# A gated mix of a long convolution and a token-mixing MLP: DFT tables laid out by group of four shifts, and a new emission order

## Chip, core and metric

The kernel runs on one core of a Trainium2 chip. The metric is the device time of one execution in microseconds. The engines are TensorE (PE, with weight loads as PEld), VectorE (DVE), ScalarE (ACT), GpSimd (POOL) and SyncE (SP); here SP issues every DMA. Shown are 13 runs of the kernel before, and one profiled execution.

## What is computed

For an input x of 2048 tokens by 640 channels, the kernel computes `g*a + (1-g)*b`, with g a sigmoid gate for each token. Branch a is a long convolution; branch b is a mixer with two residual steps:

```python
x = A_q
g = sigmoid((x * gate_w).sum(-1, keepdims=True))
# a
k_shift = sum over t<4 of shifted k * shift_k
kv = k_shift * v
y = irfft(rfft(kv, 2S) * rfft(ssm_k, 2S))[:S]
a = q * (y + kv * ssm_D)
# b
h = gelu(layernorm(x) @ w1)
hs = concat(four channel groups of h, shifted by 1, -1, 2, -2 tokens) @ w2
x1 = x + hs
b = x1 + gelu(layernorm(x1) @ w3) @ w4
```

Inputs and output are bf16; the transform in the reference is f32.

## The kernel before

**Tiling.** Tokens are laid out as 128 partitions by 16 slabs (`T1 = 16`), so that a slab is a tile of 128 tokens by 640 channels. The slabs of x are held in QX and updated in place. Branch b runs in four chunks of four slabs; branch a transforms along the tokens in two steps, one over the partitions of each slab and one over the slabs.

**Nodes.** The work is cut into named nodes, each with its engine, its dependencies and its buffers. The text of `ORDER` lists all nodes in the order in which they are emitted; `h1.6.1/P/2/1`, say, is node `h1.6.1` on PE, with PSUM bank 2 and store buffer 1. `Plan.order` reads this text and emits each node at its place. An engine works through its own nodes in that order, and waits wherever one needs something that isn't ready. The costs given to `pl.add` and `pl.dma` (`rate`, `iss`, `ndesc`) are for the planner that wrote the text; no instruction depends on them.

**Branch b.**
- `st0`, `rs0`, `xn0` (L497 to L530): layernorm statistics, their power, the normalized slab. `tr`/`te` transpose it on PE, or `xt` (L537) by DMA, into XNT.
- `W1.c.n` (L574): first matmul, five column groups for chunk c; `g1` (L581) is its gelu. `gt.c` (L588) is the gate's matmul and `z` its evacuation, `gate0` to `gate2` the sigmoid.
- `mx.c.gi` (L609 to L614): copies of 32 partitions that shift the rest of the four channel groups; they run on POOL or on DVE.
- `W2.s` (L663) and `add.s` (L670): second matmul of a slab and its sum into QX, which also gives the second layernorm's sums. Then `st1`, `rs1`, `xn1`, and `xt1` (L537).
- `W3.c.f` (L749), `g2` (L753), `W4.s.j` (L762), `w4e.s.j` (L768): the last two matmuls, the gelu between them, and the sum into QX. `xo.s` scales a slab by 1-g. The load of w4 (L733) waits for `m3n`, since it overwrites the place in which M3 is made.

**Branch a.**
- `ang`, `and`, `sin`, `abs` (L391 to L405) make the first DFT table F1, with half h (0 and 1, the table's two halves of 128 columns) and slab s. They work in four groups of four slabs; each group is two sines and an abs on ScalarE. The angles are kept in the tile of the inverse table, I1, until it is filled.
- `trh`/`trhe` transpose the convolution's kernel. `h1.s.h` (L718) is its first DFT step for slab s and half h, two matmuls; `he` evacuates them and `hw` (L727) stores two slabs to GHD in DRAM.
- `km`, `ka`, `kv` (L806 to L818): the short convolution of k and the product with v, on DVE. `x1.s.h` (also L718), `xe`, `xw` do for kv what `h1`, `he`, `hw` do for the kernel, to GXD.
- `m3i`, `m3b`, `m3c` (L432 to L448), `m3d` (L452), `m3s` (L454), `m3n` (L456): the small second-step table M3, made on POOL but for m3b and m3d on DVE and a sine on ScalarE.
- `rh`/`rx` (L862) read GHD and GXD back in another order; `h2`, `x2` (L835) are the second step, `sw` swaps halves, `pq` (L895) multiplies, `pv` goes back; `ve` and `vw` (L912) store to VD.
- `tri0`, `tri1` (L824): two DMA transposes that fill I1 from F1, one for each half. `rv` (L919), `rq` (L923), `iv` (L931), `ye`, `y`, `ya` (L941 to L951) and `st` (L953): read VD, inverse first step, times q and gate, sum, and store of a slab.

PSUM has eight banks, and there are rings of buffers for the stores (sg, 3), the gelu outputs (gt, 4) and more. A node that takes a buffer waits for the users of the one that had this place before.

**What the change touches.** F1 and I1 are tiles of 128 partitions by [2 halves, 16 slabs, 128 columns]. The sines of group g write columns of every second place in both halves:

```python
F1 = big.tile([P, 2, T1, P], BF16, name="F1")
out=F1[:, :, 4 * g:4 * g + 4, :].rearrange("p h a (j c) -> p a h j c", c=2)[:, :, :, :, x]
```

In `step1` the matmul reads `F1[:, h, s, :]`. Both transposes wait for all eight sines and for m3n, and each inverse node waits for both transposes.

Of the kernel before, what the change touches and what calls it, by code (L numbers as in the profile page):

```python
# [34 lines left out]
class Plan:  # L35
# [17 lines left out]
    def dma(self, name, fn, nbytes, deps=(), bufs=(), rate=370.0, iss=360.0, ndesc=128):  # L53
        return self.add(name, {"SP": iss}, fn, deps, bufs, None, nbytes, rate, iss, ndesc)
# [31 lines left out]
bpi/V q1/S is/G cs/V iw/G cw/V ang3/V and3/V sin3.1/A ang1/V and1/V sin1.1/A abs1/A ang2/V idn/G warm/P/0 h0/S trh0/P/2 q0/S  # L86
st0.0/A st0.3/V st0.2/V trhe0/A/2 ang0/V and0/V st0.1/V misc/G rs0.2/G xn0.3/V/0 xn0.2/V/1 h4/S trh4/P/4 trhe4/V/4 rs0.0/G
xn0.1/V/2 h1/S trh1/P/6 sin1.0/A trhe1/A/6 sin0.1/A abs0/A sin0.0/A tr0.0.2/P/0/0/1/0 xn0.0/V/0 and2/V te0.0.2/V/0/0 sin2.1/A
h3/S trh3/P/2 tr0.0.0/P/4/0/0/2 te0.0.0/V/4/0 q3/S st0.7/V st0.6/V w1/S W1.0.3/P/0/0 W1.0.2/P/1/0 w1m/G trhe3/V/2 q2/S st0.5/V
st0.4/A h2/S g1.0.3/A/0 trh2/P/6 g1.0.2/A/1 trhe2/V/6 rs0.6/G q7/S xn0.6/V/1 xn0.7/V/0 rs0.4/G W1.0.0/P/2/0 xn0.4/V/2  # L90
W1.0.4/P/3/0 g1.0.4/A/3 mx0.0/G kz/G/0 h1.1.1/P/4/0 he.1.1/A/4/0 h1.5.0/P/6/1 he.5.0/V/6/1 tr0.1.2/P/0/1/1/0 te0.1.2/A/0/1
ka/S/0 g1.0.0/A/2 xn0.5/V/0 q5/S st0.11/V gw/S gt.0/P/3/0 w2b2/S h1.5.1/P/4/1 he.5.1/A/4/1 q6/S q4/S st0.12/A tr0.1.0/P/6/1/2/0
te0.1.0/V/6/1 st0.10/V m3i3/G rs0.10/G W1.0.1/P/0/0 h1.4.0/P/4/1 he.4.0/A/4/1 h1.4.1/P/6/1 he.4.1/V/6/1 g1.0.1/A/0 W1.1.0/P/1/1
g1.1.0/A/1 W1.1.4/P/2/1 g1.1.4/A/2 h1.2.0/P/6/2 he.2.0/A/6/2 st0.9/V z0/V/3 w2b0/S w2a/S kb/S/0 drow/S h1.0.1/P/4/0
he.0.1/A/4/0 h1.0.0/P/0/0 he.0.0/A/0/0 W1.1.1/P/3/1 w2b3/S cjb/S w2b1/S hw2/S/1 mx1.1/G xn0.10/V/1 xt0.2.2/S/0/1 st0.8/V
xn0.11/V/0 xt0.2.3/S/0/0 kc/S/0 st0.15/V h1.3.1/P/6/2 he.3.1/A/6/2 h1.3.0/P/4/2 he.3.0/V/4/2 abs3/A g1.1.1/A/3 W1.1.3/P/2/1
g1.1.3/A/2 h1.1.0/P/0/0 h1.2.1/P/6/2 m3i0/G he.2.1/A/6/2 rs0.8/G xn0.8/V/2 xt0.2.0/S/0/2 st0.13/V he.1.0/V/0/0 W1.1.2/P/4/1
g1.1.2/A/4 hw0/S/0 xn0.9/V/1 mx1.0/G xt0.2.1/S/0/1 h1.7.0/P/2/1 he.7.0/A/2/1 st0.14/V gt.1/P/5/1 z1/V/5 h1.7.1/P/6/1
he.7.1/A/6/1 abs2/A sin3.0/A sin2.0/A mx1.3/G mx0.2/G W2.5/P/0 add5/V/0 hw1/S/2 rs0.12/G xn0.13/V/0 xn0.12/V/2 xt0.3.1/S/1/0
st1.5/A h1.6.0/P/2/1 mx0.1/G h1.6.1/P/4/1 he.6.0/A/2/1 he.6.1/V/4/1 hw3/S/1 W2.3/P/6 add3/V/6 st1.3/A W2.2/P/0 add2/V/0 st1.2/A  # L100
cj3/G cj1/G m3i5/G W2.4/P/4 add4/V/4 rs0.14/G xn0.15/V/1 xt0.3.0/S/1/2 xt0.3.3/S/1/1 h1.12.1/P/6/0 W1.2.1/P/0/0 m3b/V
g1.2.1/A/0 gt.2/P/1/0 h1.13.0/P/2/0 W1.2.2/P/4/0 W1.2.4/P/5/0 km0.0.3/V/0/0 xn0.14/V/0 st1.4/A xt0.3.2/S/1/0 g1.2.2/A/4
g1.2.4/A/5 z2/V/1 he.12.1/V/6/0 h1.11.0/P/0/2 he.11.0/A/0/2 he.13.0/V/2/0 h1.13.1/P/6/0 he.13.1/A/6/0 W1.2.3/P/4/0
h1.12.0/P/2/0 h1.9.1/P/0/1 he.12.0/A/2/0 he.9.1/A/0/1 W1.2.0/P/5/0 v0/S h1.8.1/P/6/1 gt.3/P/0/1 he.8.1/A/6/1 h1.10.1/P/2/2
he.10.1/A/2/2 cj2/G cj0/G hw6/S/0 km0.0.2/V/0/0 ka0.0.2/V/0/0 rs1.2/G xn1.2/V/2 xt1.0.0/S/0/2 km0.0.1/V/0/1 km0.0.0/V/0/0
ka0.0.1/V/1/0 z3/V/0 ka0.0.0/V/0/0 g1.2.0/A/5 g1.2.3/A/4 W1.3.2/P/1/1 h1.9.0/P/6/1 h1.10.0/P/2/2 he.9.0/A/6/1 he.10.0/A/2/2
W1.3.4/P/0/1 g1.3.4/A/0 kv0/V/0 mx2.3/V km0.1.3/V/0/0 xn1.3/V/1 rs1.4/G xn1.5/V/0 mx2.1/G km0.1.2/V/0/1 mx1.2/V km0.1.1/V/0/0
W1.3.1/P/4/1 g1.3.1/A/4 g1.3.2/A/1 h1.14.1/P/6/0 he.14.1/A/6/0 W1.3.3/P/0/1 h1.8.0/P/2/1 g1.3.3/A/0 h1.15.1/P/4/0 he.15.1/A/4/0
xn1.4/V/2 ka0.1.2/V/1/0 he.8.0/V/2/1 W1.3.0/P/1/1 h1.14.0/P/6/0 he.14.0/A/6/0 ka0.1.1/V/0/0 gate0/V m3i2/G mx2.0/G W2.9/P/4
h1.11.1/P/2/2 g1.3.0/A/1 m3i4/G m3i1/G m3c/G he.11.1/A/2/2 gate1/A mx3.1/G m3d/V m3s/A km0.1.0/V/0/1 mx3.2/G m3n/G add9/V/4  # L110
h1.15.0/P/6/0 W2.6/P/0 he.15.0/A/6/0 w3/S W2.8/P/2 gate2/V ka0.1.0/V/1/0 xo2/A add6/V/0 W2.7/P/4 kv2/V/0 xt1.0.3/S/0/0 add8/V/2
xt1.0.1/S/0/1 xt1.0.2/S/0/2 W3.0.3/P/0/0/0 W3.0.4/P/1/0/1 W3.0.2/P/2/0/0 g2.0.2/A/2/0 g2.0.3/A/0/0 st1.6/A W3.0.9/P/3/0/2
g2.0.4/A/1/1 W3.0.8/P/6/0/2 g2.0.8/A/6/2 W3.0.1/P/7/0/0 W3.0.7/P/0/0/1 g2.0.9/A/3/2 W3.0.5/P/1/0/1 W3.0.11/P/6/0/2 g2.0.5/A/1/1
g2.0.1/A/7/0 g2.0.11/A/6/2 add7/V/4 st1.7/A k1/S/1 km1.0.3/V/1/0 km1.0.2/V/1/0 ka1.0.2/V/0/0 km1.0.1/V/1/1 ka1.0.1/V/1/0
km1.0.0/V/1/0 ka1.0.0/V/0/0 v1/S st1.9/A xo4/A kv4/V/0 km1.1.3/V/1/0 km1.1.2/V/1/1 ka1.1.2/V/1/0 km1.1.1/V/1/0 km1.1.0/V/1/1
ka1.1.1/V/0/0 mx3.0/G mx2.2/G mx3.3/G W3.0.0/P/1/0/0 W2.11/P/4 W3.0.6/P/2/0/1 W2.12/P/6 ka1.1.0/V/1/0 kv6/V/0 W3.0.10/P/3/0/2
g2.0.7/A/0/1 add11/V/4 rs1.6/G st1.8/A g2.0.6/A/2/1 hw4/S/1 k2/S/0 km2.0.3/V/0/0 w4/S km2.0.2/V/0/0 v3/S W2.10/P/4 v2/S
ka2.0.2/V/0/0 hw5/S/2 tri0/S rs1.8/G xn1.9/V/0 xo9/V g2.0.0/A/1/0 g2.0.10/A/3/2 st1.11/A xo3/A W4.3.0/P/0/0/1/2
W4.3.1/P/1/0/1/2 x1.3.0/P/2/1 xe.3.0/A/2/1 add10/V/4 st1.10/A xn1.6/V/1 xn1.8/V/2 xt1.1.2/S/1/2 xt1.1.3/S/1/0 km2.0.1/V/0/1
ka2.0.1/V/1/0 w4e3.1/V/1 w4e3.0/V/0 k3/S/1 xt1.1.0/S/1/1 km2.0.0/V/0/0 ka2.0.0/V/0/0 rs1.10/G W4.2.0/P/4/0/1/2 w4e2.0/V/4  # L120
x1.0.1/P/2/2 xe.0.1/A/2/2 kv8/V/0 W2.13/P/0 add13/V/0 xn1.11/V/2 km2.1.3/V/0/0 km2.1.2/V/0/1 xn1.7/V/0 W4.4.1/P/2/0/1/2
x1.2.0/P/4/1 xe.2.0/A/4/1 add12/V/6 ka2.1.2/V/1/0 W4.2.1/P/3/0/1/2 w4e4.1/V/2 xo11/A st1.12/A xn1.10/V/1 km2.1.1/V/0/0 st1.13/A
xo5/V x1.0.0/P/0/2 W4.5.1/P/4/0/1/2 W4.5.0/P/2/0/1/2 ka2.1.1/V/0/0 km2.1.0/V/0/1 w4e2.1/V/3 hw7/S/0 xt1.1.1/S/1/0
W4.4.0/P/5/0/1/2 w4e4.0/V/5 W3.1.2/P/3/1/3 g2.1.2/A/3/3 W3.1.7/P/5/1/0 g2.1.7/A/5/0 x1.1.1/P/6/2 W3.1.0/P/3/1/3 xe.0.0/A/0/2
xe.1.1/A/6/2 W3.1.3/P/5/1/3 g2.1.0/A/3/3 g2.1.3/A/5/3 rs1.12/G xn1.13/V/0 xo13/V ka2.1.0/V/1/0 kv10/V/0 xt1.2.0/S/0/1 tri1/S
km3.0.3/V/1/0 xt1.2.3/S/0/0 w4e5.0/V/2 km3.0.2/V/1/0 x1.1.0/P/0/2 xe.1.0/A/0/2 x1.2.1/P/6/1 xe.2.1/A/6/1 w4e5.1/V/4
ka3.0.2/V/0/0 km3.0.1/V/1/1 ka3.0.1/V/1/0 km3.0.0/V/1/0 W3.1.5/P/2/1/0 g2.1.5/A/2/0 W3.1.8/P/3/1/1 ka3.0.0/V/0/0 g2.1.8/A/3/1
xw0/S/2 x1.6.0/P/4/0 x1.3.1/P/0/1 xe.3.1/A/0/1 xw1/S/1 xt1.2.1/S/0/2 xn1.12/V/1 kv12/V/0 xo7/V km3.1.3/V/1/0 km3.1.2/V/1/1
ka3.1.2/V/1/0 xe.6.0/A/4/0 W3.1.4/P/2/1/0 g2.1.4/A/2/0 x1.7.0/P/6/0 xe.7.0/A/6/0 km3.1.1/V/1/0 x1.7.1/P/0/0 xe.7.1/A/0/0
W3.1.10/P/3/1/1 g2.1.10/A/3/1 x1.6.1/P/4/0 xe.6.1/A/4/0 xt1.2.2/S/0/1 xw3/S/0 W3.1.1/P/2/1/3 g2.1.1/A/2/3 ka3.1.1/V/0/0  # L130
x1.8.1/P/6/2 xe.8.1/A/6/2 x1.9.1/P/0/2 xe.9.1/A/0/2 x1.9.0/P/4/2 xe.9.0/A/4/2 W3.1.6/P/3/1/0 x1.8.0/P/6/2 xe.8.0/A/6/2 xw4/S/2
g2.1.6/A/3/0 x1.12.1/P/0/1 xe.12.1/V/0/1 W3.1.9/P/2/1/1 x1.13.0/P/4/1 xe.13.0/A/4/1 km3.1.0/V/1/1 x1.12.0/P/6/1 xe.12.0/V/6/1
x1.13.1/P/0/1 xe.13.1/A/0/1 xw6/S/1 ka3.1.0/V/1/0 kv14/V/0 rh1/S/0 g2.1.9/A/2/1 W3.1.11/P/3/1/1 g2.1.11/A/3/1 rh0/S/1
# [46 lines left out]
def kernel(  # L180
# [16 lines left out]
    nc = tc.nc  # L197
# [161 lines left out]
    def gt_(n, dt):  # L359
        t = GEN[:, gpos[0]:gpos[0] + 2 * n].bitcast(dt)  # L360
        gpos[0] += 2 * n
        return t

    I1f = I1.rearrange("p h t d -> p (h t d)")
    NANG = I1f.bitcast(I32)
    NABS = I1f.bitcast(F32)
    wci, wcf = gt_(P, I32), gt_(P, F32)
# [620 lines left out]
```

## Time and profile before

| | us |
|---|---|
| median of 13 runs | 236.31 |
| lowest, highest | 234.73, 239.13 |
| the profiled execution | 236.97 |
| its span (first to last instruction) | 235.2 |

| engine | busy us | share of the span |
|---|---|---|
| PE | 216.2 | 92% |
| DVE | 190.6 | 81% |
| ACT | 164.3 | 70% |
| POOL | 59.6 | 25% |

The DMA queue used by SP takes 88.9% of the span of 16 DMA engines, with 65.6 MB. The granted PE clock is 0.99 over the span. In the chain that ended last PE has 57%, DMA 17%, DVE 15%. A busy share is a mean over stages with different limits; the chain says what the end hung on. Groups of the profile are named by source line, with the tile written, an arrow, and the tiles read; tiles that share a name but for a number are shown as one. An engine's idle time has in brackets what ended it.

### The profile page before, as it was taken

To read this page: it belongs to the slowest core of one execution; us is meant where nothing else is said; L and a number is where in the kernel's file an instruction comes from. 1 tells how busy PE (TensorE), PEld (TensorE's weight loads), DVE (VectorE), ACT (ScalarE), POOL (GpSimd) and SP (SyncE) were. 2 spreads that over 40 slices of the span, in tenths; PEclk is the share of its full clock that TensorE was granted. 3 is DMA by queue.
4 is the path that set the end of the run, shared out by engine and by line. 5 is a ranking of instruction groups with operands and counts; after the bars stand their busy time and mean duration, and the time that the engine had idled before them with its cause. 6 is when DMAs were issued, how large, how long until landed. Compare 5 with 4: busy or idle time off the path is not lost.

```text
span 235.2 us, 4450 instructions
## 1 busy us (share of the span) xinstructions
PE 216.2 (92%) x1641; PEld 124.6 (53%) x1641; DVE 190.6 (81%) x342; ACT 164.3 (70%) x251; POOL 59.6 (25%) x136
## 2 busy tenths in 40 slices
PE   6769995999989999899999999999999999999970
PEld 6637453655644566655566456533346553476640
DVE  8998984599999999999984777998957896046883
ACT  5997989488756853529987971779986896645440
POOL 4444377179982344140002001000000000000000
PEclk9999998899999999999999999999999999999999
DMA  6999579459999996993879999999998954799996
GB/s 217 397 355 300 214 195 281 144 147 264 270 275 403 383 321 119 316 168 114 270 248 363 399 224 356 293 309 375 283 380 265 395 177 160 217 403 348 296 313 249
DMA packets 53029, 65.89 MB, mean 280 GB/s; under 512 B 22544, under 2 KB 39697, under 8 KB 52624
## 3 DMA queue, kind: packets, MB, share of 16 engines
q1 hardware_dynamic: 53008, 65.61, 88.9%
q8 instruction: 13, 0.21, 0.4%
q14 instruction: 8, 0.07, 0.1%
HBM read 37.03 MB, written 18.35 MB: 235 GB/s over the span
## 4 chain that ended last, share of the span: by engine, by line
PE 57%; DMA 17%; DVE 15%; ACT 3%; SPq 3%; issue 2%; POOL 1%; DVEq 0%; ACTq 0%; POOLq 0%
PE PS L749 15%; PE PS L762 13%; PE PS L574 8%; PE PS L835 8%; PE PS L718 7%; DMA CJ<-in_A_q_dram 6%; DMA RG<-in_A_ssm_k_dram 5%; PE PS L663 5%; DVE RK L811 4%; DMA RK<-GHD 3%; DMA XNT<-XN 3%; DVE RK L815 3%; DVE QX L670 2%; DVE RK L945 2%; DVE QX L951 1%
## 5 line engine op out<-in xcount | busy, mean ns | idle before, releaser
L320 ACT CAST SX<-PS 128x640 bf16<-128x640 f32 (+1 forms) x65 | 47.9, 769 | 21.6 <-PE PS L835 10.9
L762 PE MATMUL PS<-W,RG 128*128 128x320 bf16 x384 | 56.5, 300 | 1.0 <-DVE QX L768 0.7
L749 PE MATMUL PS<-XNT,W 128*128 128x512 bf16 x240 | 56.1, 380 | 0.9 <-DVE QX L670 0.7
L762 PEld LDWEIGHTS <-RG 128*128 128x128 bf16 x384 | 36.5, 98 | 20.1 <-issue 5.7
L749 PEld LDWEIGHTS <-W 128*128 128x128 bf16 x240 | 22.6, 98 | 29.1 <-issue 5.9
L753 ACT ACTIVATE RG<-PS 128x512 bf16<-128x512 f32 x48 | 27.9, 604 | 13.3 <-PE PS L749 12.9
L718 PE MATMUL PS<-KV,F 128*128 128x320 bf16 x128 | 24.8, 302 | 2.8 <-ACT F L398 2.7
L768 DVE SCALAR_TENSOR_TENSOR QX<-PS,ZG,QX 128x320 bf16<-128x320 f32 x32 | 17.1, 545 | 12.3 <-PE PS L762 12.3
L895 DVE TENSOR_TENSOR SX<-SX,R 128x2048 bf16<-128x2048 bf16 x20 | 24.0, 1220 | 2.5 <-DMA R<-R 2.2
L663 PE MATMUL PS<-R 128*128 128x320 bf16 x160 | 25.3, 311 | 0.4 <-DVE QX L768 0.2
L574 PE MATMUL PS<-XNT,R 128*128 128x512 bf16 x100 | 24.0, 379 | 1.1 <-DVE XNT L324 1.1
L324 DVE CAST SX<-PS 128x640 bf16<-128x640 f32 (+1 forms) x19 | 17.7, 942 | 4.6 <-ACT RG L503 2.2
L663 PEld LDWEIGHTS <-R 128*128 128x128 bf16 x160 | 16.3, 102 | 8.5 <-issue 1.1
L815 DVE TENSOR_TENSOR RK<-RK 128x1280 bf16<-128x1280 bf16 x24 | 20.2, 842 | 0.4
L811 DVE TENSOR_TENSOR RK<-RK,CJ 128x1280 bf16<-128x1280 bf16 x24 | 20.4, 855 | 0.0
L941 ACT ACTIVATE RK<-PS,ZG 128x640 bf16<-128x640 f32 x16 | 12.0, 792 | 11.8 <-PE PS L931 10.4
L670 DVE SCALAR_TENSOR_TENSOR QX<-PS,QX 128x640 bf16<-128x640 f32 x16 | 13.0, 819 | 8.1 <-PE PS L663 8.1
L718 PEld LDWEIGHTS <-F 128*128 128x128 bf16 x128 | 12.1, 98 | 12.0 <-ACT F L398 3.0
L320 ACT CAST KV<-PS 128x1024 bf16<-128x1024 f32 x17 | 17.0, 1019 | 1.3 <-PE PS L835 1.2
L503 ACT ACTIVATE RG<-QX 128x640 bf16<-128x640 bf16 x16 | 11.7, 733 | 6.8 <-DVE QX L670 6.7
L326 DVE TENSOR_SCALAR R<-PS 128x1024 bf16<-128x1024 f32 x10 | 12.1, 1223 | 4.2 <-PE PS L835 3.0
L574 PEld LDWEIGHTS <-R 128*128 128x128 bf16 x100 | 9.6, 98 | 10.4 <-DMA R<-in_B_w_dram 0.6
(104 smaller groups left out, 281.6 us busy)
## 6 DMA issues: line engine op xcount, KB each, us to landing
GHD<-SX SPq DMA_DIRECT2D x8, 640.0 KB, 4.1
GXD<-SX SPq DMA_DIRECT2D x8, 640.0 KB, 3.4
RK<-GHD SPq DMA_DIRECT2D x4, 1280.0 KB, 7.7
RK<-GXD SPq DMA_DIRECT2D x4, 1280.0 KB, 8.4
R<-R SPq DMA_DIRECT2D x8, 640.0 KB, 7.9
VD<-KV SPq DMA_DIRECT2D x4, 1280.0 KB, 6.0
RK<-VD SPq DMA_DIRECT2D x8, 640.0 KB, 6.3
W<-in_B_w_dram SPq DMA_DIRECT2D x2, 1920.0 KB, 12.3
```

Source lines behind the costliest of these rows:

```text
L320: nc.scalar.copy(out=o, in_=i)
L574: nc.tensor.matmul(ps(pb), lhsT=lhsT, rhs=XNT[:, xb.idx, k, :], start=(k == 0), stop=(k == DT - 1))
L663: nc.tensor.matmul(ps(pb)[:, j, 0:DH], lhsT=gst_ap(k, s), rhs=W2[:, k, j * DH:(j + 1) * DH], start=(k == 0), stop=(k == DT - 1))
L670: nc.vector.scalar_tensor_tensor(out=x, in0=ps(pb)[:, :, 0:DH], scalar=1.0, in1=x, op0=ALU.mult, op1=ALU.add, accum_out=SSM[:, s:s + 1])
L718: nc.tensor.matmul(ps(pb)[:, j, 0:DH], lhsT=F1[:, h, s, :], rhs=src[:, s, ds], start=True, stop=not dterm)
L749: nc.tensor.matmul(ps(pb), lhsT=W3[:, k, f0 * P:(f0 + 1) * P], rhs=XNT[:, xb.idx, k, :], start=(k == 0), stop=(k == DT - 1))
L753: gns.append(pl.add("g2.%d.%d" % (c, f0), {A: act_p(512)}, lambda e, f0=f0, pb=pb, gb=gb: nc.scalar.activation(out=GTP[:, gb.idx, f0 % 4, ...
L762: nc.tensor.matmul(ps(pb)[:, 0:DH], lhsT=GTP[:, gbs[f // 4].idx, f % 4, i * P:(i + 1) * P], rhs=W4[:, f, j * DH:(j + 1) * DH], start=(f == ...
L811: m = pl.add("km%d.%d.%d" % (c, u, j), {V: dve(2 * D, .52)}, lambda e, src=src, cj=cj, tb=tb: nc.vector.tensor_tensor(out=TMP[:, tb.idx].r ...
L815: prev = pl.add("ka%d.%d.%d" % (c, u, j), {V: dve(2 * D, .52)}, lambda e, tb=tb: nc.vector.tensor_tensor(out=acc, in0=acc, in1=TMP[:, tb.i ...
L835: nc.tensor.matmul(pt[64 * C:64 * C + 64, R, :], lhsT=M3[64 * R:64 * R + 64, m, :], rhs=rhs_fn(R, C), start=start, stop=stop)
L895: nc.vector.tensor_tensor(out=PQ[:, qb.idx], in0=XS[:, sb.idx].unsqueeze(1).to_broadcast([P, 2, 1024]), in1=HH[:, hhb.idx, u], op=ALU.mult)
```

## The change

The tables F1 and I1 become [4 groups, 2 halves, 4 slabs, 128 columns], so that a group of four slabs is one piece for both halves. Each transpose now covers two groups (both halves of eight slabs) instead of one half of all slabs; it waits for the four sines of its groups, and an inverse node waits only for the transpose that has its slab. The planner's spacing of a DMA issue goes from 360 to 470 ns, and that of an XNT transpose from 1230 to 1320. The text of `ORDER` is new: the place of most nodes, many buffer numbers, and the engine of some. The evacuations and statistics that change between ScalarE and DVE are about as many each way. `mx1.2` and `mx2.3` go from DVE to POOL; `cj0` goes from POOL to ScalarE. No node is added or removed.

```diff
-    def dma(self, name, fn, nbytes, deps=(), bufs=(), rate=370.0, iss=360.0, ndesc=128):
+    def dma(self, name, fn, nbytes, deps=(), bufs=(), rate=370.0, iss=470.0, ndesc=128):
...
-    F1 = big.tile([P, 2, T1, P], BF16, name="F1")
-    I1 = big.tile([P, 2, T1, P], BF16, name="I1")
+    F1 = big.tile([P, 4, 2, 4, P], BF16, name="F1")
+    I1 = big.tile([P, 4, 2, 4, P], BF16, name="I1")
...
-    I1f = I1.rearrange("p h t d -> p (h t d)")
+    I1f = I1.rearrange("p g h t d -> p (g h t d)")
...
-                out=F1[:, :, 4 * g:4 * g + 4, :].rearrange("p h a (j c) -> p a h j c", c=2)[:, :, :, :, x],
+                out=F1[:, g].rearrange("p h a (j c) -> p a h j c", c=2)[:, :, :, :, x],
...
-                            nc.tensor.matmul(ps(pb)[:, j, 0:DH], lhsT=F1[:, h, s, :], rhs=src[:, s, ds], start=True,
+                            nc.tensor.matmul(ps(pb)[:, j, 0:DH], lhsT=F1[:, s // 4, h, s % 4, :], rhs=src[:, s, ds], start=True,
...
-        out=I1[:, h], in_=F1[:, h].rearrange("p t c -> p (t c)")), P * P * T1 * 2, f1n + [m3n], [], rate=XT_RATE, iss=2060.0, ndesc=1600) for h in range(2)]
+        out=I1[:, 2 * h:2 * h + 2].rearrange("p g h t c -> p (g h t) c"), in_=F1[:, 2 * h:2 * h + 2].rearrange("p g h t c -> p (g h t c)")), P * P * T1 * 2, f1n[4 * h:4 * h + 4] + [m3n], [], rate=XT_RATE, iss=2060.0, ndesc=1600) for h in range(2)]
...
-                        nc.tensor.matmul(ps(pb)[:, j, 0:DH], lhsT=I1[:, h, s, :], rhs=VX[:, xb.idx, h, s % 2, j * DH:(j + 1) * DH],
+                        nc.tensor.matmul(ps(pb)[:, j, 0:DH], lhsT=I1[:, s // 4, h, s % 4, :], rhs=VX[:, xb.idx, h, s % 2, j * DH:(j + 1) * DH],
...
-            pe = pl.add("iv%d" % s, {PE: 4 * 136}, f_inv, [ld] + i1n, [pb, xb], mode="f")
+            pe = pl.add("iv%d" % s, {PE: 4 * 136}, f_inv, [ld, i1n[s // 8]], [pb, xb], mode="f")
```

Of the order, the places that the next section speaks of, each with nodes around it left out (the letter after the slash is the engine, S for SP and G for POOL):

```
before  abs3/A he.7.0/A gt.1/P h1.7.1/P he.7.1/A abs2/A sin3.0/A sin2.0/A W2.5/P st1.5/A h1.6.0/P h1.6.1/P W2.3/P st1.3/A W2.2/P W2.4/P h1.12.1/P
after   he.7.0/A gt.1/P abs2/A abs3/A sin3.0/A sin2.0/A h1.6.0/P W2.5/P h1.7.1/P he.7.1/A h1.6.1/P W2.3/P W2.2/P st1.3/A cj0/A W2.4/P h1.12.1/P
before  st1.5/A mx2.3/V rs1.4/G mx2.1/G mx1.2/V mx2.0/G m3i1/G m3c/G m3d/V add9/V add6/V add8/V W3.0.3/P W3.0.8/P W3.0.7/P add7/V
after   mx2.1/G mx2.0/G st1.5/A rs1.4/G mx1.2/G m3i1/G mx2.3/G add6/V add7/V m3c/G m3d/V add9/V W3.0.7/P W3.0.8/P add8/V h1.15.0/P W3.0.3/P
before  m3c/G mx3.1/G m3d/V m3s/A mx3.2/G m3n/G mx3.0/G mx2.2/G mx3.3/G
after   m3c/G m3d/V m3s/A mx3.2/G mx3.3/G mx2.2/G mx3.1/G mx3.0/G m3n/G
before  k1/S v1/S hw4/S k2/S w4/S v3/S v2/S hw5/S tri0/S xt1.1.2/S xt1.1.3/S k3/S xt1.1.0/S hw7/S xt1.1.1/S xt1.2.0/S tri1/S xt1.2.3/S xw0/S
after   k1/S v1/S k2/S hw5/S w4/S v2/S k3/S hw4/S xt1.1.1/S xt1.1.0/S xt1.1.3/S xt1.1.2/S hw7/S tri0/S v3/S tri1/S xw0/S
```

## The prediction

> **What bounds it now.** I read the busy rows first, then the chain of waits, then PE's timeline with its idle times, then the engines that PE waits for. Of the page (part 2):
>
> ```profile
> PE   6769995999989999899999999999999999999970
> DVE  8998984599999999999984777998957896046883
> PEclk9999998899999999999999999999999999999999
> DMA  6999579459999996993879999999998954799996
> ```
>
> One slice is 5.9 us. PE is full from slice 4 to 38 but for a dent at slices 7 and 8, and there alone its clock falls. DVE is full from 47 to 121 us, the DMA engines from 120 to 172. So nearly every us of PE idle before 224 us is a us of the span; what else must not be late is DVE up to 121.
>
> To place things I add, engine by engine in table order, the mean step (start to next start) of each kind: a W1 or W3 group 1.08 us, W2 1.36, W4 1.68, a pair of L718 0.27; on DVE L670 0.75, L811 0.80, L815 0.74, L530 0.36. Time in the trace minus this sum is what the engine has lost. PE has lost 5.95 us at 35 us, 11.90 at 68.5 (start of W3), 13.1 at 102, 15.6 at 197, 17.7 at its end.
>
> The dent, in PE's timeline (start, length; idle and releaser in brackets), ScalarE's timeline, and the window sums (PE, PEld, DVE, ACT, POOL, then clock, DMA share, GB/s):
>
> ```profile
> 36.30 0.43 PE L718 MATMUL PS<-KV,F 128*128 128x320 bf16 x2
> 39.43 0.71 PE L718 MATMUL PS<-KV,F 128*128 128x320 bf16 x2 [2.70 <-ACT F L398]
> 39.93 5.70 PE L663 MATMUL PS<-R 128*128 128x320 bf16 x30
> ...
> 68.46 0.81 PE L749 MATMUL PS<-XNT,W 128*128 128x512 bf16 x3 [0.69 <-DVE QX L670]
> ```
> ```profile
> 36.51 1.28 ACT L398 ACT_TABLE_LOAD   x1
> 37.80 1.57 ACT L398 ACTIVATE F<-I,BPI 128x512 bf16<-128x512 f32 x2
> ```
> ```profile
> 36.00:39.40 3.40, 0.73 (x6) 0.29 (x3) 1.55 (x4) 3.37 (x5) 3.32 (x7) 1.00 1.15 281
> 39.40:43.00 3.60, 3.57 (x14) 2.01 (x15) 0.92 (x2) 1.22 (x3) 0.27 (x1) 0.53 0.69 234
> ```
>
> The pair after the gap is `h1.6.1`. It needs table group 1, whose sines were done at 10.6 us. It waits for the sines of groups 2 and 3 (37.80 to 39.37), which it doesn't read: with F1 as [half, slab], group 2 runs from half 0, slab 8 to half 1, slab 11, and half 1, slab 6 lies between these ends.
>
> **1. F1 by group: the gap goes.** In the new layout a group is one piece. In the built order of the changed kernel the weight load of `h1.6.1` no longer waits for ScalarE. The first pair that reads group 3, `h1.12.1`, comes after three W2 groups: PE work ahead 35.14 + 5.95 lost = 41.1 us, while ScalarE's sines end near 40 (`he.7.0`, two abs, table load 1.28, two sines, as before). Gone are 2.70 us and the slow clock. The clock record is at half for 3.41 us, so 1.71 us more (30 matmuls of L663 took 5.49 us in the chain, 4.08 at full clock; the rest on the pair). **4.4 us.** The Trainium skill, "TensorE: Matmul & The Clock Gate" (What's actually happening), has the clock halve after an idle window of about 3.4 us; by that a 2.70 us gap keeps it, and the gain would be 2.7. The row shows 0.53 after 0.73 busy us in 3.40. I take the row: 4.4.
>
> What hides behind the gap: xt0.2, add5, add3, z1 and sg buffers. Walking the new order from 18 to 62 us with 5.95 lost, each PSUM bank is free 0.2 to 2 us before PE asks; the last transpose for W1.2 lands near 38.5 against 41.4. DVE there idled with PE (2.2, 1.9, 0.6, 0.5 us), so it moves up too.
>
> **2. Two edge copies (mx1.2, mx2.3) from DVE to POOL, ahead of m3c.** The copies' line (min/median/max ns), then the ends of m3c on POOL's timeline:
>
> ```profile
> L609 POOL COPY R<-R x14: 397/612/1172, 21.6 to 102.0; 32x512 bf16<-32x512 bf16 x10, 32x384 bf16<-32x384 bf16 x2, 32x256 bf16<-32x256 bf16 x2
> ...
> L609 DVE COPY R<-R x2: 300/302/305, 56.9 to 59.5; 32x512 bf16<-32x512 bf16 x2
> ```
> ```profile
> 53.58 0.37 POOL L432 CAST W<-W 128x5 f32<-128x5 int32 x1
> ...
> 63.53 0.46 POOL L448 TENSOR_SCALAR W<-W 128x64 f32<-128x64 f32 x1
> ```
>
> DVE saves 0.6 us. POOL pays: a copy takes 0.6 us at 30 us but 1.06 to 1.17 at 50 to 53, beside DVE's two-input L811 and L815. The skill's "SBUF — State Buffer" (SBUF: two separate sides) says why this move is poor: POOL and a DVE op with two SBUF inputs hold one port pair exclusively. By uncontended copies it costs 1.2 us, by these rows 2.2; I take 2.2. m3c (L432 to L448) spans 10.4 us here. New start: PE work ahead of `h1.11.1` 42.67 + 5.95 = 48.6, its evacuation and st1.5 on ScalarE to 50.7, rest of rs1.4 1.3, copy 1.1, iota 0.2, copy 1.1: 54.5, so m3c ends at 64.9. DVE by its sum reaches m3d (waiting on m3c) at 63.7: it waits 1.2. Queued behind are add9 and add8 (to 66.7), and bank 0 of add8 is what `W3.0.3` wants at 65.0. PE loses about 1.8 us there, where before it lost the 0.69 shown. Between ends: 0 if POOL starts 1.2 earlier, 4 if contention stretches it. By the row a gap of 0.69 kept the clock and 2.70 did not; at 1.8 I take it as kept, 1.7 more is in the range. So PE's loss at `W3.0.3` is 7.9 in place of 11.90: **a gain of 4.0 so far**, 4.4 plus the smaller waits of before, less this one.
>
> **3. W4's load.** SP's timeline:
>
> ```profile
> 67.87 0.38 SPq L733 DMA_DIRECT2D W<-in_B_w_dram  x1
> 68.34 7.26 SPq L795 DMA_DIRECT2D KV<-in_A_v_dram  x2
> 75.66 0.42 SPq L727 DMA_DIRECT2D GHD<-SX  x1
> 76.12 11.41 SPq L824 DMA_TRANSPOSE I<-F  x1
> ...
> 100.92 1.98 SPq L824 DMA_TRANSPOSE I<-F  x1
> ```
>
> w4 waits for m3n. The new table puts all mx3 and mx2.2 copies (4.6 us in the trace) before m3n (1.5): done at 71.0 instead of 67.9. Behind w4 on SP stand v2, k3, hw4. Before, w4 landed 15.2 us after issue, behind k1, v1, hw4, k2. Now k1, v1, k2, hw5 leave from 59 us, when the xt1.0 transposes are out, and are in near 71.4 (steps of their landings before: 4.7 for k1 and v1, 2.7 for k2, 1.6). Then w4 runs alone: 2 us to start plus its 6.3: 79.4. `W4.3.0` has 72.38 of PE work ahead, + 7.9 = 80.3. **Covered by 0.9 us; nothing.** A later m3n costs PE one for one.
>
> **4. tri0 and tri1** move behind xt1.1 and hw7, and each reads two groups. tri0's 11.41 us on SP came with a full queue (DMA share 1.03 from 70 to 85); tri1 took 1.98. At about 90 us, with k3 and hw4 in, I take 2 each. Before xw0 there are then 5 us to spare; at 11.41 PE would wait some 2. The inverse reads them over 100 us later: per-half waits there bring nothing. k3 leaves 10 us earlier and its wait (before: 6.7 us on xt1.1 in the chain, behind k3) goes, but PE lost only 0.70 by it.
>
> **5. 64 to 121 us: DVE.** Ahead of kv14 stand 107.75 us of DVE work against 108.90: xo5, xo7, xo9, xo13 leave, evacuations come. DVE keeps the 4 us. PSUM banks are tight at W4.4.1, x1.11.0, x1.4.0 and W2.1 (0.4 to 0.9 us): up to 1 us lost, about what before lost in other places (0.2 + 0.70 + 0.1). Nothing.
>
> **6. After kv14.** rh1 left when kv14 ended (121.27); so the full DMA stretch moves up whole. From `W3.2.2` on PE's work ahead agrees within some us, from `pv.1.2` exactly; the same nine groups cover VD's round trip, and the end (W4.0.1, iv13, st13) is the same. The tail from 203 us moves 9.6 MB (at 390 GB/s 24.6 us): it shifts, it doesn't shrink. Spacing numbers (`iss`) are read by the planner alone: nothing.
>
> **Sum:** 236.97 − 4.0 = 233.0 for an execution like the profiled one (span 235.2); that lay 0.66 above the median of 13, 236.31. **232.3 us.**
>
> **Rivals.** (a) Half the gain: m3c stretched by contention or w4 1 to 2 us late; for it, that both covers are about 1 us; against, that everything ahead on POOL and SP moves up as well. Gain 1 to 2.5: 234.5. (b) Slower: w4 issued at 71 still needs 15.2 us because k2's and hw5's transfers slip to it; landing 86.2, PE waits 5.9, and the clock halves (1.7): net +3.6, 239.9. It decides from a landing at 84.3. Against it: the 15.2 was queue, not transfer. (c) No wait at m3d, banks all free: gain 6, 230.3. (d) The layout helps but the later DMA stretch is the bound and stays: same, 236.3; against it, that its start hangs on kv14.
>
> **Numbers.** As forecast 0.55 (230.8 to 233.6), (a) 0.20, (b) 0.13, (c) 0.07, (d) 0.05. 0.3%, or 0.7 us, is about what a measurement of this kernel can tell from no change: faster 0.81, same 0.06, slower 0.13. Range 229.8 to 236.0: all but (b) and some of (d).
>
> **To be seen after:** no gap near 36 us and no clock under 1.0 until the end; a PE wait for L670 near 65 us; DVE idle before L452; L733 issued near 71 and landed before PE's first L762; tri issues of 2 us; PE's end near 224.5. Wrong if PE waits at the first L762, or if rh1 isn't issued by 118.

## The result, and the profile after

| | before | after |
|---|---|---|
| median, us | 236.61 (48 runs) | 231.6 (11 runs) |
| lowest, highest | 234.73, 239.37 | 230.6, 234.5 |

The ratio is 0.9805, with a 95% interval of 0.9778 to 0.9833: 4.6 us faster, with 232.3 forecast. In two later batches the changed kernel gave 232.54 and 231.34 (6 runs each, ratios 0.9829 and 0.9779). The medians are of all runs; the ratios leave out the few executions that took over 1.5% longer than the fastest of their kernel. The profiled execution after, 234.5 us with a span of 231.6, is the slowest of its eleven. Ahead of its tail it had half clock twice for 3.41 us, at 10.19 and at 64.80; the two later profiles of the same kernel had none and one such stretch.

The busy rows of the page after (40 slices of 5.8 us):

```profile
PE   6789999999879999999999999999999999999950
DVE  8889979979969999999997677998648894076593
PEclk9889999999979999999999999999999999999997
DMA  6999889989999995899989979999999963799896
```

The dent of slices 7 and 8 is gone from PE and DVE, and so is that of slices 8 and 9 from the DMA engines. A smaller one stands at slices 11 and 12 (58 to 70 us), with the only low clock between the kernel's start and its tail. In the chain that ended last, PE has 75% of the span where it had 57%, and DVE 5% where it had 15%:

```profile
PE 75%; DMA 11%; DVE 5%; ACT 4%; issue 2%; SPq 1%; ACTq 0%; DVEq 0%
```

**The old gap.** PE's timeline, then ScalarE's, of the changed kernel (start, length), then the window sums (PE, PEld, DVE, ACT, POOL, clock, DMA share, GB/s):

```profile
35.24 1.52 PE L663 MATMUL PS<-R 128*128 128x320 bf16 x10
36.60 0.71 PE L718 MATMUL PS<-KV,F 128*128 128x320 bf16 x4
37.14 4.24 PE L663 MATMUL PS<-R 128*128 128x320 bf16 x30
...
64.86 3.96 PE L749 MATMUL PS<-XNT,W 128*128 128x512 bf16 x10 [2.18 <-DMA XNT<-XN]
```
```profile
36.83 1.28 ACT L398 ACT_TABLE_LOAD   x1
38.12 1.59 ACT L398 ACTIVATE F<-I,BPI 128x512 bf16<-128x512 f32 x2
```
```profile
36.00:39.40 3.40, 3.40 (x27) 2.46 (x26) 3.25 (x6) 3.37 (x5) 2.91 (x6) 1.00 1.11 232
39.40:43.00 3.60, 3.60 (x26) 2.29 (x25) 3.60 (x9) 3.58 (x8) 0.96 (x4) 1.00 1.02 310
```

ScalarE loads its table and makes the last two sines when it did before (38.12 to 39.71), but PE no longer stands meanwhile: the two pairs at 36.60 (`h1.7.1` and `h1.6.1`) run into thirty matmuls of W2. Those take 4.24 us, where before they took 5.70 at half clock. In the first window PE is busy 3.40 us of 3.40 instead of 0.73. `W2.4` starts at 39.86 instead of 44.10, 4.24 us earlier.

**The new gap.** 2.18 us before the first group of W3, put down to a transpose into XNT and not to DVE. POOL's timeline (the copies, first and last row of m3c) and DVE's at `m3d`:

```profile
53.92 0.68 POOL L609 COPY R<-R 32x512 bf16<-32x512 bf16 x1
...
55.04 0.94 POOL L609 COPY R<-R 32x512 bf16<-32x512 bf16 x1
56.05 0.22 POOL L432 CAST W<-W 128x5 f32<-128x5 int32 x1
...
64.26 0.56 POOL L448 TENSOR_SCALAR W<-W 128x64 f32<-128x64 f32 x1
```
```profile
64.31 0.26 DVE L452 TENSOR_SCALAR W<-W 128x192 int32<-128x192 int32 x1 [0.37 <-POOL W L447]
```

The queue of SP, and two pieces of the chain of waits (start, length, what):

```profile
51.92 0.57 SPq L675 DMA_DIRECT2D W<-in_B_w_dram  x1
54.85 4.15 SPq L537 DMA_TRANSPOSE XNT<-XN  x2
...
70.89 0.38 SPq L733 DMA_DIRECT2D W<-in_B_w_dram  x1
...
94.43 3.65 SPq L824 DMA_TRANSPOSE I<-F  x1
...
98.75 4.19 SPq L824 DMA_TRANSPOSE I<-F  x1
```
```profile
57.69 6.93 DMA XNT<-XN
64.62 0.25 issue
```

The load of w3, 1920 KB, leaves at 51.92 and lands at 61.80. The last two transposes of the chunk leave after it and land after it, at 63.86 and 64.62; the last took 6.93 us from issue. PE had finished W2 at 62.7. The clock was at half from 64.80 to 68.22, so this gap cost 2.18 us and 1.7 more, in this execution.

### The profile page after: what moved, and what is told of

Same layout as the page of the kernel before. It is cut to its first block, busy times and chain, and to the rows that moved or that the text cites. A ratio compares the mean times of both kernels' runs of the same rounds, so it can differ in the third digit from the quotient of the medians.

```text
span 231.6 us, 4458 instructions
## 1 busy us (share of the span) xinstructions
PE 215.5 (93%) x1641; PEld 126.4 (55%) x1641; DVE 188.6 (81%) x340; ACT 165.4 (71%) x252; POOL 60.4 (26%) x137
## 4 chain that ended last, share of the span: by engine, by line
PE 75%; DMA 11%; DVE 5%; ACT 4%; issue 2%; SPq 1%; ACTq 0%; DVEq 0%
PE PS L749 20%; PE PS L762 18%; PE PS L574 9%; PE PS L718 8%; PE PS L835 7%; PE PS L663 7%; DMA RG<-in_A_ssm_k_dram 3%; DMA XNT<-XN 3%; DMA CJ<-in_A_q_dram 3%; DMA RK<-VD 2%; PE PS L696 2%; DVE RK L945 2%; DVE QX L951 1%; ACT RK L941 1%; PE PS L545 1%
## 5 line engine op out<-in xcount | busy, mean ns | idle before, releaser
L320 ACT CAST SX<-PS 128x640 bf16<-128x640 f32 (+1 forms) x62 | 46.4, 777 | 18.7 <-PE PS L835 10.4
L749 PE MATMUL PS<-XNT,W 128*128 128x512 bf16 x240 | 57.5, 388 | 2.2 <-DMA XNT<-XN 2.2
L762 PE MATMUL PS<-W,RG 128*128 128x320 bf16 x384 | 56.0, 299 | 0.1
L762 PEld LDWEIGHTS <-RG 128*128 128x128 bf16 x384 | 36.6, 98 | 18.8 <-issue 5.1
L718 PE MATMUL PS<-KV,F 128*128 128x320 bf16 x128 | 23.9, 299 | 0.0
L324 DVE CAST SX<-PS 128x640 bf16<-128x640 f32 (+1 forms) x22 | 19.9, 911 | 4.5 <-PE PS L718 3.1
L663 PE MATMUL PS<-R 128*128 128x320 bf16 x160 | 23.4, 299 | 0.0
L663 PEld LDWEIGHTS <-R 128*128 128x128 bf16 x160 | 15.7, 98 | 6.3
L574 PEld LDWEIGHTS <-R 128*128 128x128 bf16 x100 | 9.6, 98 | 10.2 <-issue 1.1
L530 DVE TENSOR_SCALAR XN<-QX,MV,RS 128x640 bf16<-128x640 bf16 x32 | 14.2, 456 | 0.6 <-issue 0.6
L523 POOL TENSOR_TENSOR RS<-VE,NHALF 128x2 f32<-128x2 f32 x16 | 13.8, 865 | 1.3
L835 PEld LDWEIGHTS <-M 64*64 64x64 bf16 x320 | 7.6, 105 | 11.7 <-issue 7.0
```

Source lines behind the costliest of these rows:

```text
L320: nc.scalar.copy(out=o, in_=i)
L324: nc.vector.tensor_copy(out=o, in_=i)
L574: nc.tensor.matmul(ps(pb), lhsT=lhsT, rhs=XNT[:, xb.idx, k, :], start=(k == 0), stop=(k == DT - 1))
L663: nc.tensor.matmul(ps(pb)[:, j, 0:DH], lhsT=gst_ap(k, s), rhs=W2[:, k, j * DH:(j + 1) * DH], start=(k == 0), stop=(k == DT - 1))
L718: nc.tensor.matmul(ps(pb)[:, j, 0:DH], lhsT=F1[:, s // 4, h, s % 4, :], rhs=src[:, s, ds], start=True, stop=not dterm)
L749: nc.tensor.matmul(ps(pb), lhsT=W3[:, k, f0 * P:(f0 + 1) * P], rhs=XNT[:, xb.idx, k, :], start=(k == 0), stop=(k == DT - 1))
```

## Experiments

The first batch of four ran beside one set of runs of the kernel before (median 236.44), the second beside another (236.78), the third beside a third (237.19).

### The layout alone, the order alone

Three kernels ask whether `h1.6.1` was held by sines that it doesn't read, and which half of the change frees it. The first is the changed code with the old text of `ORDER`:

```diff
 ORDER = """
-bpi/V q1/S is/G cs/V iw/G cw/V ang3/V and3/V sin3.1/A idn/G warm/P/0 ang1/V and1/V sin1.1/A ang2/V abs1/A st0.3/V
+bpi/V q1/S is/G cs/V iw/G cw/V ang3/V and3/V sin3.1/A ang1/V and1/V sin1.1/A abs1/A ang2/V idn/G warm/P/0 h0/S
...
```

> The order of before with the new layout of F1 and I1 (and the transposes by group). Theory A, the gap at h1.6.1 came from a wait on sines of other groups, and the layout is what takes it away: no gap and no half clock at 36 to 43 us, PE 4.4 us earlier at W2.4; part of it is lost again at the start of W3 (m3c, or the landing of the last transpose), so 2.5 to 4.5 us under before. Theory B, the gap came from where ScalarE stood in the order, and the new order took it away: the gap stays, within 0.7 us of before.

Measured: 232.63 us, ratio 0.9849 (0.9797 to 0.9901). The second is the old code with the new text:

```diff
 ORDER = """
-bpi/V q1/S is/G cs/V iw/G cw/V ang3/V and3/V sin3.1/A ang1/V and1/V sin1.1/A abs1/A ang2/V idn/G warm/P/0 h0/S
+bpi/V q1/S is/G cs/V iw/G cw/V ang3/V and3/V sin3.1/A idn/G warm/P/0 ang1/V and1/V sin1.1/A ang2/V abs1/A st0.3/V
...
```

> The order of after with the old layout. Theory A: h1.7.1 stands behind the sines of groups 2 and 3 in this order, so PE idles from 36.6 to about 39.7 us and its clock halves: 4 to 5 us over after, within 1 us of before. Theory B: no gap, within 0.7 us of after.

Measured: 236.0 us, ratio 0.9999 (0.9966 to 1.0032). PE's timeline of the layout alone, then of the order alone, at the same place:

```profile
35.87 0.71 PE L718 MATMUL PS<-KV,F 128*128 128x320 bf16 x4
36.41 4.24 PE L663 MATMUL PS<-R 128*128 128x320 bf16 x30
```
```profile
38.80 1.25 PE L718 MATMUL PS<-KV,F 128*128 128x320 bf16 x4 [2.98 <-ACT F L398]
39.83 3.91 PE L663 MATMUL PS<-R 128*128 128x320 bf16 x20
```

With the new layout the pairs run through under either order. With the old layout the new order has a gap of 2.98 us, one pair earlier (`h1.7.1`), and half clock after it (20 matmuls of L663 in 3.91 us). `h1.6.0` is emitted behind the same sines in both old kernels and ran without a wait, at 36.30 us before and at 34.02 here, ahead of the sines. It reads half 0, slab 6, which lies ahead of the sines' first address (half 0, slab 8); `h1.6.1` and `h1.7.1` read half 1, slabs 6 and 7, between first and last. So the wait went by the range from first to last address and not by the whole tile.

The third leaves the old layout and each engine's own order as they are. Only the place of an abs, two sines and the statistics after them on ScalarE is moved in the text, to behind the pair that waited for the sines:

```diff
-abs2/A sin3.0/A sin2.0/A mx1.3/G mx0.2/G W2.5/P/0 add5/V/0 ... st1.5/A h1.6.0/P/2/1 mx0.1/G h1.6.1/P/4/1
+mx1.3/G mx0.2/G W2.5/P/0 add5/V/0 ... h1.6.0/P/2/1 mx0.1/G h1.6.1/P/4/1 abs2/A sin3.0/A sin2.0/A st1.5/A
```

> The kernel before, old layout; only the two sines (and the abs and statistics beside them on ScalarE) are emitted after h1.6.1, so that each engine's own order is the same and only the wait of h1.6.1 on them goes. Theory A: as with the layout alone, no gap at 36 us, 2.5 to 4.5 us under before. Theory B, or if the layout does something else (weight loads, transposes): no change.

Measured: 234.02 us, ratio 0.9874 (0.9816 to 0.9931). A read that is emitted ahead of a write doesn't wait for it, and the gap is gone without the layout:

```profile
36.95 0.71 PE L718 MATMUL PS<-KV,F 128*128 128x320 bf16 x4
37.49 4.24 PE L663 MATMUL PS<-R 128*128 128x320 bf16 x30
```

So the wait was a false one, and removing it in either way is most of the gain: 3.6 us by the layout alone, 3.0 us by the place in the text alone. The profile of the latter then lost 1.99 us at the start of W3, to a transpose, with half clock behind it. How much the new order adds to the layout (0.9849 against 0.9805) lies within the intervals.

### What holds the start of W3

The forecast had DVE's `add8`, behind `m3d` and m3c, hold it. The fourth kernel takes the two copies back to DVE:

```diff
-mx1.2/G ... mx2.3/G
+z3/V/1 mx1.2/V mx2.3/V
```

> The kernel after, with mx1.2 and mx2.3 back on DVE (after z3). POOL's m3c starts some 2 us earlier, w4 is issued near 69. If add8 behind m3d is what holds the start of W3 (as forecast): 1 to 1.8 us faster than after. If the landing of the last XNT transpose at 64.6 is what holds it (as the trace of after says): the same to 0.6 us slower, since DVE's xn1.5 and with it that transpose is 0.66 us later.

Measured: 231.99 us, ratio 0.9804 (0.9747 to 0.9862), the same as the changed kernel's. `m3d` ran earlier (63.71 instead of 64.31), but W3 still waited for a transpose, now 0.60 us:

```profile
62.92 2.32 PE L749 MATMUL PS<-XNT,W 128*128 128x512 bf16 x9 [0.60 <-DMA XNT<-XN]
```

The next one moves the load of w3 ahead of all four transposes:

```diff
-hw6/S/0 ... xt1.0.0/S/0/2 ... xt1.0.1/S/0/1 w3/S
+hw6/S/0 w3/S ... xt1.0.0/S/0/2 ... xt1.0.1/S/0/1
```

> The changed kernel with one move on SP's queue: the load of w3 goes from its place after xt1.0.1 to right after hw6, ahead of all four xt1.0 transposes; no other engine's order changes. In the trace of the changed kernel w3 was issued at 51.92 and landed at 61.80, xt1.0.2 and xt1.0.3 were issued at 54.85 and 57.69 and landed at 63.86 and 64.62, and PE stood 2.18 us at its first L749 until an XNT transpose landed, with half clock for 3.4 us after it. Theory 1 (the transposes queue behind w3's bytes): w3 lands near 58, the last transpose 2 to 4 us after its issue, near 61.5; PE's gap at the first L749 is 0.7 us or less and no half clock follows in any case; 230.2 to 231.0 us. Theory 2 (the forecast's: m3c and add8 hold the start of W3): the gap stays between 1 and 2 us, its releaser DVE; no change, 231.6. Theory 3 (the landings of xt1.0 vary from run to run whatever stands before them): no change in the median, 231.6, but a gap that differs from profile to profile.

Measured: 232.86 us, ratio 0.9861 (0.9806 to 0.9917). PE's timeline, then DVE's (with its idle time in brackets), then the chain of waits:

```profile
63.35 0.38 PE L749 MATMUL PS<-XNT,W 128*128 128x512 bf16 x1 [1.96 <-DVE QX L670]
```
```profile
58.13 0.45 DVE L530 TENSOR_SCALAR XN<-QX,MV,RS 128x640 bf16<-128x640 bf16 x1 [2.15 <-DMA XNT<-XN]
...
62.48 0.81 DVE L670 SCALAR_TENSOR_TENSOR QX<-PS,QX 128x640 bf16<-128x640 f32 x1
```
```profile
47.25 10.85 DMA XNT<-XN
58.10 0.03 issue
58.13 0.45 DVE XN L530
```

The first expectation came true in its first half only: w3 landed at 57.37 and the last transpose at 61.34, 3.3 us earlier than in the first profile of the changed kernel. But now the first transpose, `xt1.0.0`, queues behind w3 and lands 10.85 us after its issue, at 58.10 instead of 54.19. It reads buffer 2 of XN, into which `xn1.5` writes next. DVE stood 2.15 us for that buffer, everything behind it came later, and `add6` freed bank 6, which the first group of W3 takes, at 63.29. The gap is as long as before and has another cause. Both moves together:

```diff
-hw6/S/0 ... xt1.0.1/S/0/1 w3/S ... mx1.2/G ... mx2.3/G
+hw6/S/0 w3/S ... xt1.0.1/S/0/1 ... z3/V/1 mx1.2/V mx2.3/V
```

> The run before with also mx1.2 and mx2.3 back on DVE after z3, as in e4_mx_on_dve. Theory 1: both things that could hold W3's start are gone, gap 0.3 us or less; if DVE's add8 is what comes next once the transposes are early, this is 0.5 to 1 us faster than the run before it: 229.5 to 230.5. If the copies matter to nothing (as e4_mx_on_dve said while the transposes were late), it equals the run before it.

Measured: 233.29 us, ratio 0.983 (0.9778 to 0.9882). `add6` again: DVE stood 1.23 us for the same buffer, PE 1.22 and 0.66 us at W3. No gain over the changed kernel, which ran beside them unaltered:

> The changed kernel itself, unaltered, beside the others: the base for their ratios and a second profile of it. Ratio 0.980 as in the result, 231.6 us. If the gap at the first L749 is a matter of landings that vary, this profile shows it with another length than 2.18 us, and the half clock only if it is above 1 us or so.

Measured: 232.54 us, ratio 0.9829 (0.9787 to 0.9871). Its gap in this profile, then in a third profile of the same kernel, taken with the last batch:

```profile
64.05 2.32 PE L749 MATMUL PS<-XNT,W 128*128 128x512 bf16 x9 [1.93 <-DVE W L452]
```
```profile
62.77 2.32 PE L749 MATMUL PS<-XNT,W 128*128 128x512 bf16 x9 [0.66 <-DVE KV L818]
...
79.71 1.79 PE L762 MATMUL PS<-W,RG 128*128 128x320 bf16 x12 [0.51 <-DMA W<-in_B_w_dram]
```

In the first of them the engine named makes nothing that this group of W3 takes; the last transposes landed at 63.08 and 63.81, and PE went on at 64.05. So the length differs from run to run, 2.18, 1.93 and 0.66 us, with these landings. Half clock had been expected from about 1 us on; after 1.93 us it did not come.

Eight profiles have w3 in its place between the second and the third transpose: these three, the kernel with the copies on DVE, and the four kernels that follow. In all eight the last transpose lands 2.77 to 2.91 us after w3, and PE starts W3 0.24 or 0.25 us after that, whatever engine is named. What varies is the landing of w3, 7.96 to 9.87 us after its issue; why it varies is not shown. The last line shows what takes the gap's place where it is short: PE then comes to `W4.3.0` earlier and waits for w4 (0.51 us here; 0.48 and 0.84 us in the kernels with more PE and with less DVE work below, after gaps of 0.58 and 0.43).

### How thin the cover of w4 is

> The changed kernel with k3's load moved ahead of w4 on SP's queue: k3 waits for its buffer until 79.7 us (km1.1.0's end), so w4 is issued near 80.0 instead of 70.89 and lands near 89. PE asked for W4.3.0 at 82.44 in the trace. Step 3 of the forecast (a later w4 costs PE one for one once the cover of 1 to 2 us is used up): a gap of 6 to 7 us at the first L762, half clock for 3.4 us behind it (1.7 us more), and half or less of it regained before kv14, since DVE bounds up to 121 us and goes on with km and ka meanwhile: 235 to 240 us. If there is slack that the forecast did not see (DVE, not PE, sets the end of this stretch, and PE catches up), under 233.5.

```diff
-k1/S/1 ... v1/S ... k2/S/0 hw5/S/1 ... w4/S v2/S ... k3/S/1 hw4/S/2
+k1/S/1 ... v1/S ... k2/S/0 hw5/S/1 ... k3/S/1 w4/S v2/S ... hw4/S/2
```

Measured: 242.54 us, ratio 1.0267 (1.0214 to 1.0319), 10.0 us over the changed kernel beside it. PE's timeline, DVE's, and the window sums:

```profile
88.94 3.36 PE L762 MATMUL PS<-W,RG 128*128 128x320 bf16 x12 [9.99 <-DMA W<-in_B_w_dram]
```
```profile
92.42 0.55 DVE L768 SCALAR_TENSOR_TENSOR QX<-PS,ZG,QX 128x320 bf16<-128x320 f32 x1 [9.80 <-PE PS L762]
```
```profile
78.00:89.00 11.00, 1.01 (x8) 0.62 (x7) 4.51 (x8) 3.32 (x7) 1.87 (x5) 0.65 0.92 318
89.00:96.00 7.00, 7.00 (x31) 4.03 (x31) 3.55 (x6) 0.00 (x0) 0.00 (x0) 0.58 0.48 157
```

w4 landed at 88.90 instead of 79.11, 9.8 us later, and as much was paid, more than the 235 to 240 us expected. PE's clock stayed at half until 94.94, by estimate 3 us more of PE time (half of the 6.0 us of work at that clock); against that, the gaps of the kernel beside it (1.93 and 0.88 us) are 0.51 us and none here. So "one for one" holds for the sum and not for each term. The expectation that DVE would go on with km and ka was wrong: `w4e3.0`, an evacuation of W4, stands ahead of them on DVE, which stood 9.80 us too. PE and DVE stop together. PE asked for w4 at 78.95 here; in the changed kernel it lands at 79.1 to 80.2. There is no slack left in front of this load when W3 starts with a short gap.

### Which engine sets the pace up to kv14

The last three put work on one engine or take it off.

```diff
-                    prev = pl.add("km%d.%d.3" % (c, u), ..., lambda e, src=src, cj=cj: nc.vector.tensor_tensor(
-                        out=acc, in0=src(), in1=cj, op=ALU.mult), ...)
+                    prev = pl.add("km%d.%d.3" % (c, u), ..., lambda e, src=src, cj=cj, c=c, u=u: [nc.vector.tensor_tensor(
+                        out=acc, in0=src(), in1=cj, op=ALU.mult) for _ in range(2 if (c, u) in ((2, 1), (3, 0), (3, 1)) else 1)][-1], ...)
```

> The changed kernel with three DVE operations done twice (km2.1.3, km3.0.3, km3.1.3, 0.81 us each between 92 and 110 us): 2.4 us more DVE work ahead of kv14. In the last profile of the changed kernel PE was busy 51.7 of the 53 us from 64 to 117 and DVE 51.0, so either may set kv14. If DVE sets it (step 5 of the forecast): kv14 and the end come 2.0 to 2.4 us later. If PE sets it and DVE has slack: 0 to 1 us later.

Measured: 234.57 us, ratio 0.9899 (0.9866 to 0.9931).

```diff
-                for k in range(DT):
+                for k in list(range(DT)) * (2 if c == 1 and f0 in (2, 8) else 1):
                     nc.tensor.matmul(ps(pb), lhsT=W3[:, k, f0 * P:(f0 + 1) * P], rhs=XNT[:, xb.idx, k, :],
```

> The changed kernel with two PE groups done twice (W3.1.2 and W3.1.8, 1.08 us each near 95 us): 2.2 us more PE work ahead of kv14. PE work is total work of the kernel as well. If DVE alone sets kv14 and the DMA stretch that hangs on kv14 sets the end: under 1 us later, since PE makes it up while it waits after kv14. If PE sets it, before or after kv14: 2.2 us later.

Measured: 235.25 us, ratio 0.9916 (0.9882 to 0.9951).

```diff
-                        out=acc, in0=acc, in1=TMP[:, tb.idx].rearrange("p (t d) -> p t d", t=2), op=ALU.add)
+                        out=acc[:, :, 0:w], in0=acc[:, :, 0:w], in1=TMP[:, tb.idx].rearrange("p (t d) -> p t d", t=2)[:, :, 0:w], op=ALU.add)
```

Here w is 32 for ka2.1.1, ka3.0.1 and ka3.1.1, and 640 for the others.

> The changed kernel with three of DVE's additions in the short convolution (ka2.1.1, ka3.0.1, ka3.1.1) done on 32 of every 640 columns only, the rest of these three sums left out: about 2.2 us less DVE work between 97 and 114 us, nothing else changed. If DVE alone sets kv14 and kv14 sets the end: 2 us faster. If PE is as late as DVE there (both are over 96% busy): kv14 moves by at most 1 us and the end by 0 to 1 us.

Measured: 231.98 us, ratio 0.9753 (0.9698 to 0.9808). The base of the three:

> The changed kernel itself, unaltered, as the base for these three: ratio 0.98, 231.6 to 232.5 us.

Measured: 231.34 us, ratio 0.9779 (0.9729 to 0.9829). From each profile, the start of the last row of L818 on DVE (kv14) and of the last row of L931 on PE, in us:

| | kv14 | last L931 | from one to the other |
|---|---|---|---|
| before | 120.42 | 227.92 | 107.50 |
| after, the three profiles | 117.10, 115.98, 115.81 | 224.51, 223.53, 222.28 | 107.41, 107.55, 106.47 |
| DVE + 2.4 us | 117.53 | 225.12 | 107.59 |
| PE + 2.2 us | 117.59 | 226.49 | 108.90 |
| DVE - 2.2 us | 114.18 | 223.63 | 109.45 |
| w4 late | 126.52 | 233.33 | 106.81 |

More work on DVE costs about what it takes (ratio up by 0.012, 2.8 us), and so does more work on PE (0.0137, 3.2 us, with the 2.2 us added well within the intervals). Less work on DVE brings nothing that these runs can tell (ratio down by 0.0026, within the intervals): kv14 comes 1.6 us earlier than in the profile of its base, and the end does not, since the stretch behind kv14 is longer by 3.0 us. So neither engine is the bound by itself: PE's own work is as late as kv14's data. That reading rests on one profile of each kernel and on these ratios.

## Why the prediction was right

**Step 1, the gap.** Right in cause and size: 4.4 us forecast, `W2.4` came 4.24 us earlier, and the gap was shown to be a false wait by three kernels. The slow clock went with it, as the row said: 4.24 us came and not the 2.70 of the gap alone.

**Step 2, the copies and the start of W3.** The net of 4.0 us held, against 4.6 us measured, but not by its reasoning. The forecast had m3c end at 64.9 (64.82), DVE wait 1.2 us at `m3d` (0.37), `add8` end at 66.7 (66.05) and PE lose about 1.8 us at `W3.0.3`. PE lost 2.18, 1.93 and 0.66 us in three profiles, at `W3.0.7`, to a transpose. The term that was left out is the queue on SP: w3's 1920 KB goes out between the second and the third transpose. That the size came near is luck. The two copies cost POOL 0.68 and 0.94 us, 1.6 together, between the 1.2 and the 2.2 that were weighed; back on DVE they change no time.

The clock there was taken as kept, with 1.7 us more in the range. It was halved after 2.18 us in the first profile and kept after 1.93 and 0.66 in the others: the range was needed.

**Step 3, w4.** Issued at 70.89 (71 forecast), landed at 80.24, 79.11 and 79.67 in the three profiles (79.4). From issue to landing w4 took 9.35, 8.77 and 8.37 us where 2 + 6.3 was taken; the 2 us to start is an estimate that no row of the trace before carries, where the quickest transfers land 2.4 us after issue. A cover of about 1 us was right as a size, but not as a promise: PE asked 2.2 us after the landing in the first profile, and in the third it waited 0.51 us at its first L762. That was named as a sign of being wrong; it came true there at no cost that shows, since the gap at W3 was shorter by more. One for one was right for the sum, by the kernel with w4 late: 10.0 us for 9.8. Rival (b) was thus a real danger that this order just escapes.

**Step 4, tri0 and tri1.** 3.65 and 4.19 us on SP, not 2 each, so the 5 us to spare before xw0 shrank by 3.8 and PE saw nothing of it: in the profiled execution no PE gap stands between 69 and 121 us.

**Step 5, up to kv14.** "DVE keeps the 4 us": kv14 came 3.3 to 4.6 us earlier in the three profiles. That DVE bounds this stretch is half of it; by the last three kernels PE bounds it as well. The gap at 36 us held both (DVE was busy 1.55 us of 3.40 in it, and 3.25 after), so its removal moved both.

**Step 6, after kv14.** The stretch from kv14 to the last L931 is 107.50 us before and 107.41 in the profile after: everything moved up by what kv14 did. rh1 was issued at 117.95, just inside the mark of 118; PE's last row ends at 225.2 in the profiled execution, against 224.5, and at 223.0 in the fastest profile. The tail's 9.6 MB are 9.9 by the trace before (307 GB/s over 32.2 us); nothing hangs on it.

**The rivals.** (a), half the gain, had the right place in part: m3c was not stretched, but a cover of about 1 us was used up. (c), no wait there at all, is what a short gap comes near to: the third profile, with 0.66 us, took 230.77 us against 230.3. (d), the later DMA stretch as a bound that stays, is out by step 6.

## What to carry to other kernels

Where one tile is written in strided pieces, a reader of one piece can be made to wait for the writers of others: here each piece counted as if it ran from its first address to its last (`h1.6.0` outside this range ran, `h1.6.1` inside it waited). Look for an engine that waits for an instruction whose data it doesn't read, then make each writer's piece contiguous, or emit the reader first. Where two engines are both full, a stall that stops both is the one to remove first: here its removal alone brought 3.6 us in one kernel and 3.0 in another, while a saving of 2.2 us on one of them brought nothing that the runs could tell. And before a large load is moved up on a queue, look at what small transfers stand behind it and whose buffers these hold.

## What the runs showed of the hardware

**A short idle can halve PE's clock.** Half clock for 3.41 us followed gaps of 2.98 (the order alone), 2.70 (before), 2.18 (after), 1.99 (sines emitted later) and 1.96 us (w3 first) in the middle of the kernel, but not 1.93 (after, second profile), 1.84 (more DVE work) and shorter ones; near the start it followed 1.68 us (after) and not 1.63 (less DVE work). So the length alone doesn't decide. The clock of each profile changes only at steps of 3.41 us, counted from a first record that lies at 5.19 to 7.78 us, elsewhere in each. What tells the cases apart better is PE's busy time in the 3.41 us ahead of such a step. In the fourteen profiles, up to 224 us, the clock fell after 0.71 us (before, 36.06 to 39.47), 0.72, 1.08, 1.29 (after, 61.39 to 64.80) and 1.42; it never fell after more than 1.73; from 1.43 (second profile, kept) to 1.73 (after, 6.78 to 10.19, fell) it went both ways. The Trainium skill, "TensorE: Matmul & The Clock Gate" (What's actually happening), calls the window free-running; the differing first records agree with that. Its "after ≥1 idle window", read as a window without work, does not hold here: PE was busy 0.71 to 1.73 us in every such window.

**Transposes behind a load wait for its bytes.** The last transpose landed 6.93 us after its issue behind w3, and 6.68 us in the second profile, each 2.8 to 2.9 us after w3 itself; the first one, put behind w3, took 10.85 us where it had taken 5.65, and landed 0.73 us after w3. Which of them is late is a matter of the place on the queue, and moves the wait to another engine.
